# Sixteen units of a linear-attention kernel, each computed in two halves of 64 tokens instead of one of 128

## The chip, the cores and the metric

The kernel runs on one core of a Trainium2 chip. The metric is device time of one execution, in microseconds (us). The core's engines are named as the profile names them: PE (TensorE, matrix multiplication; PEld is its weight load), DVE (VectorE), ACT (ScalarE), POOL (GpSimd) and SP (SyncE, which issues most DMAs). A matmul has a stationary operand (`lhsT`, the weights loaded first) and a moving one (`rhs`); the moving operand's free size is called its columns here.

## The reference

A linear attention with a decaying state, and an ELU feed-forward layer on its output. B, H, S, D = 4, 8, 768, 48; d_model = 384, d_ff = 2048.

```python
state = np.zeros((B, H, D, D))
for t in range(S):
    kt, vt, rt = (k[:, :, t], v[:, :, t], r[:, :, t])
    cur = np.einsum('bhd,bhe->bhde', u[None] * kt, vt)
    y[:, :, t] = np.einsum('bhd,bhde->bhe', rt, state + cur)
    state = w[None, :, :, None] * state + np.einsum('bhd,bhe->bhde', kt, vt)
x = y.transpose(0, 2, 1, 3).reshape(B * S, H * D)
h = x @ w_in
g = np.where(h > 0.0, h, np.exp(np.minimum(h, 0.0)) - 1.0)
return g @ w_out
```

## The kernel before

The 768 tokens are cut into six blocks of 128 (n = 0 to 5). A block with one batch entry is a unit (n, b), so there are 24 units. The feed-forward layer takes a block of all four batch entries at once, 512 columns, in 16 steps f: `hidden` ("hid", L1031) multiplies 128 of the 2048 d_ff rows of the weights with the block's x into a PSUM tile `ps_h`, ACT and DVE make the ELU of it ("neg", "elu", "gh", "gl"), and `project` ("proj", L1075) adds its product to the output sums two steps later. Its operands are split in a high and a low part, so that a step has 9 matmuls of 512 columns for each of the two. While the steps of block n run, the units of block n + 1 are computed between them.

A unit in its closed form, for 8 heads as 4 pairs a of 2 heads i (head i of a pair lies on partitions 64i to 64i+47, `ROWS[i]`):

- scores: k times r, 128 keys by 128 queries for each head, with the decay multiplied into r (powers of w) and k (inverse powers);
- DVE copies the scores through a triangular mask (`copy_predicated`, "pa", "pb", L849) into the tile `a`, whose diagonal was laid there before by POOL ("Dp", L842) and ACT ("Eq", four instructions, L838);
- outputs y, in PSUM tiles `ps_y`: the state before the block times r, plus v times `a`; ACT and DVE split y into the high and low part of x ("xh", "xl", L949, L951);
- added state: k times v over the block's 128 tokens; DVE adds it to the decayed state ("ns", L939), which POOL had decayed ("sw", L750).

Units of blocks 2 to 5 (16 of the 24) are put on PE by `insertion` ("AY"), after "hid" and before "proj" of steps 16, 20, 23, 26, 29, 33 and so on, every fourth step to 73. Such an insertion holds the scores of one unit and the outputs and added state of the unit before; the first (step 16) holds scores alone, the last (step 77) outputs alone, and in the units of block 5 there is no added state. The strings `FIRST` and `LATER` are the order of each step; "paA+1" stands for "one step after the unit's scores", "nsY+0" for "in the step of its outputs". Every engine works off its queue in that order.

PE works with parts of its array in small matmuls: a matmul of 48 or 64 contraction rows and 32 stationary columns takes a part of 64 rows and 32 columns, and eight such parts can hold different matmuls at once. The insertion before has these groups: 32 matmuls of scores with 48 x 32 weights and 128 columns (L792); 8 of state times r, 48 x 32 and 128 columns (L807); 4 more with 128 x 32 (L812); 16 of v times `a`, 128 x 32 and 128 columns (L824); 16 of added state, 128 x 32 and 48 columns (L924). The trace has two matmul records and two weight loads for each of these fp32 matmuls, and one of each for a matmul of the feed-forward layer.

Of the kernel before, what the change touches and what calls it, by code (L numbers as in the profile page):

```python
# [8 lines left out]
F32 = mybir.dt.float32  # L9
F32R = mybir.dt.float32r  # L10
I32 = mybir.dt.int32
# [19 lines left out]
ROWS = [slice(i * DP, i * DP + D) for i in range(2)]  # L31

FILL = DP - D
Q = P // HP
W_LOW, W_HIGH = 0.8, 1.2
WARM = 7
EARLY = (0, 6)
# [29 lines left out]
class Kernel:  # L67
# [87 lines left out]
    def pair(self, a):  # L155
        return slice(a * Q, (a + 1) * Q)

# [253 lines left out]
    def stages(self, n, f):  # L411
        return [(f - t, 1, b) for b, t in enumerate(BEGIN) if n == 0 and -1 <= f - t < 4]

    def units_at(self, times, step):
        return [divmod(2 * B + j, B) for j, t in enumerate(times) if t == step]

# [11 lines left out]
    def step(self, n, f):  # L428
        nc = self.nc

        k = f + 2 if n == 0 else NF + 1
# [3 lines left out]
        last = divmod(n * NF + f - (1 if (n, f) < EARLY else 2), NF)  # L435
# [31 lines left out]
            "mr": lambda n, b: self.gather_blocks(n, b),  # L467
            "br": lambda n, b: self.decay_moved(n, b, 0),
            "bk": lambda n, b: self.decay_moved(n, b, 1),
        }  # L470
        layer = {
            "hid": lambda: self.hidden(n, f, self.rest_of(n, f)),
# [13 lines left out]
            "st": lambda: self.store(last[0]) if last[1] == NF - 1 and last[0] in self.acc else None,  # L486
            "out": lambda: self.store_next(),
            "third": lambda: self.third_slot() if (n, f) == (0, 14) else None,
            "AY": lambda: self.insertion(now),
        }  # L490
        now = n * NF + f
        for op in (LATER if n else FIRST).split():
# [3 lines left out]
            if op[-2] in "+-":  # L496
                name, times = op[:-3], {"A": SCORES, "Y": OUTPUTS, "T": TURNS}[op[-3]]
# [5 lines left out]
            name, stage = op[:-1], -1 if op[-1] == "x" else int(op[-1])  # L503
# [230 lines left out]

    def key_rest(self, n, b, eng=None):

        if n + 1 == NCH:
            return
        k = self.raw[n, b][1][:, :, 0:D]
        (eng or self.nc.gpsimd).tensor_mul(k, k, self.rev[:, :, 0:D])  # L740
        if self.general:
            self.decay_state(n, b)
# [10 lines left out]
            )  # L753

    def own_state(self, b, i):
        return self.state[b][ROWS[i], :, i * D : (i + 1) * D]

    def scores(self, n, b):
        un = self.units[n, b]
# [14 lines left out]
    def insertion(self, now):  # L774

        new, old = (self.units_at(t, now) for t in (SCORES, OUTPUTS))
        if not new:
            for at in old:
                self.outputs(*at)
            return  # L780
        nc, un = self.nc, self.units[new[0]]
        un["pa"] = [self.bank("a") for _ in range(2)]
        was = self.units[old[0]] if old else None
        if was:
            was["py"] = [
                self.ps.tile([P, T], F32, tag="h", name="ps_y", bufs=2), self.bank("y"),
            ]

        for a in range(HP):
# [6 lines left out]
        if not was:  # L796
            return
        self.by_state(*old[0])
        self.by_keys(*old[0])
        self.added_state(*old[0])  # L800
# [357 lines left out]
```

## Time and profile before

| | |
|---|---|
| time, three runs | 501.12, 502.05 and 502.75 us; median 502.05 |
| span of the profiled execution, first to last instruction | 500.2 us |
| median less that span | 1.85 us |
| PE, PEld busy | 98%, 81% of the span |
| DVE, ACT, POOL busy | 61%, 48%, 21% |
| mean granted clock of PE | 0.997 of full speed |

The profile comes from one execution, on which no other time than the span is shown; what lies around it is taken as the 1.85 us by which the median exceeds it. Busy time of PE counts the modelled length of each record, and records of matmuls overlap, so a busy PE may still be slower than it could be: start times have to be read, not only busy shares.

### The profile page before, as it was taken

To read this page: it belongs to the slowest core of one execution; us is meant where nothing else is said; L and a number is where in the kernel's file an instruction comes from. 1 tells how busy PE (TensorE), PEld (TensorE's weight loads), DVE (VectorE), ACT (ScalarE), POOL (GpSimd) and SP (SyncE) were. 2 spreads that over 40 slices of the span, in tenths; PEclk is the share of its full clock that TensorE was granted. 3 is DMA by queue.
4 is the path that set the end of the run, shared out by engine and by line. 5 is a ranking of instruction groups with operands and counts; after the bars stand their busy time and mean duration, and the time that the engine had idled before them with its cause. 6 is when DMAs were issued, how large, how long until landed. Compare 5 with 4: busy or idle time off the path is not lost.

```text
span 500.2 us, 12118 instructions
## 1 busy us (share of the span) xinstructions
PE 490.4 (98%) x5013; PEld 404.0 (81%) x5013; DVE 304.7 (61%) x533; ACT 240.9 (48%) x458; POOL 107.2 (21%) x142
## 2 busy tenths in 40 slices
PE   8999999999999999999999999999999999999995
PEld 7787778777888888888887888888878878899994
DVE  7899988875676647657556665474674343433332
ACT  3377766744445443544445435444454353444442
POOL 7623332341131331130321321301011000000000
PEclk9999999999999999999999999999999999999998
DMA  9999987483364652563523625514443000010001
GB/s 139 233 215 180 225 208 189 88 156 87 96 125 109 123 127 44 119 138 60 109 61 73 149 67 111 136 44 90 113 74 89 10 1 2 8 33 24 2 0 68
DMA packets 108453, 49.11 MB, mean 98 GB/s; under 512 B 89442, under 2 KB 104292, under 8 KB 108388
## 3 DMA queue, kind: packets, MB, share of 16 engines
q1 hardware_dynamic: 96292, 43.52, 39.6%
q10 hardware_dynamic: 12096, 4.72, 4.0%
q8 instruction: 41, 0.67, 0.6%
q14 instruction: 24, 0.20, 0.1%
HBM read 35.12 MB, written 13.11 MB: 96 GB/s over the span
## 4 chain that ended last, share of the span: by engine, by line
PE 85%; DMA 4%; DVE 4%; SPq 3%; ACT 2%; issue 1%; DVEq 0%; ACTq 0%
PE ps_acc L1075 38%; PE ps_h L1031 36%; PE ps_a L792 4%; PE ps_y L824 3%; DMA stage<-in_moe_w_out_dram 2%; PE ps_y L812 1%; SPq L212 1%; PE ps_y L924 1%; DMA stage<-in_moe_w_in_dram 1%; PE ps_y L807 1%; ACT wide L571 1%; DMA r_t<-in_r_dram 1%; SPq L169 1%; SPq L165 1%; PE ps_a L768 0%
## 5 line engine op out<-in xcount | busy, mean ns | idle before, releaser
L1031 PE MATMUL ps_h<-x,wh 128*128 128x512 f32 (+1 forms) x582 | 180.5, 391 | 1.3 <-ACT x L899 1.0
L1075 PE MATMUL ps_acc<-g,wh 128*128 128x512 f32 x480 | 165.8, 400 | 0.0
L1046 DVE SCALAR_TENSOR_TENSOR ps_h<-g,ps_h 128x512 f32<-128x512 f32 x96 | 66.8, 696 | 133.5 <-ACT g L1041 133.2
L1031 PEld LDWEIGHTS ps_h<-x,wh 128*128 128x128 f32 x582 | 108.7, 188 | 24.7 <-ACT x L899 1.3
L1040 ACT ACTIVATE g<-ps_h 128x512 f32<-128x512 f32 x96 | 57.4, 598 | 133.8 <-PE ps_h L1031 123.7
L1031 PE MATMUL ps_h<-x,wl 128*128 128x512 f32 (+1 forms) x291 | 113.9, 391 | 0.0
L1075 PEld LDWEIGHTS ps_acc<-g,wh 128*128 128x128 f32 x480 | 90.1, 188 | 21.9 <-issue 0.8
L1075 PE MATMUL ps_acc<-g,wl 128*128 128x512 f32 x240 | 93.6, 390 | 0.0
L1054 DVE SCALAR_TENSOR_TENSOR g<-ps_h,g 128x512 fp32r<-128x512 f32 x96 | 66.3, 691 | 40.2 <-ACT g L1052 35.9
L1052 ACT ACTIVATE g<-ps_h 128x512 fp32r<-128x512 f32 x96 | 57.6, 600 | 67.4 <-DVE ps_h L1046 67.2
L1031 PEld LDWEIGHTS ps_h<-x,wl 128*128 128x128 f32 x291 | 54.6, 188 | 12.7
L1041 ACT ACTIVATE g<-g 128x512 f32<-128x512 f32 x96 | 60.7, 632 | 3.0
L842 POOL TENSOR_TENSOR a<-ident,diag 128x512 f32<-128x512 f32 x20 | 20.9, 1046 | 154.2 <-PE ps_y L924 78.2
L1075 PEld LDWEIGHTS ps_acc<-g,wl 128*128 128x128 f32 x240 | 45.1, 188 | 9.0
L676 POOL TENSOR_TENSOR tb<-rk,qw 128x512 f32<-128x512 f32 x16 | 20.7, 1296 | 69.5 <-DMA rk<-blocks 53.8
L1075 PE MATMUL ps_acc<-wh,g 128*128 128x384 f32 x128 | 35.3, 339 | 0.0
L849 DVE COPY_PREDICATED a<-mask,ps_a 128x512 f32<-128x512 int32 x40 | 29.4, 734 | 0.0
L838 ACT ACTIVATE a<-ident,diag 128x128 f32<-128x128 f32 x80 | 25.4, 393 | 0.0
L1075 PEld LDWEIGHTS ps_acc<-wh,g 128*128 128x128 f32 x128 | 23.4, 187 | 1.1 <-issue 0.4
L571 ACT ACTIVATE wide<-stage 128x768 f16<-128x768 bf16 (+1 forms) x18 | 17.9, 992 | 11.2 <-DMA stage<-in_moe_w_in_dram 8.3
L949 ACT CAST x<-ps_y 128x256 fp32r<-128x256 f32 (+1 forms) x40 | 10.8, 324 | 22.8 <-DVE state L939 21.3
L1075 PE MATMUL ps_acc<-wl,g 128*128 128x384 f32 x64 | 21.6, 337 | 0.0
(114 smaller groups left out, 440.0 us busy)
## 6 DMA issues: line engine op xcount, KB each, us to landing
blocks<-tb SPq DMA_DIRECT2D x64, 128.0 KB, 2.3
rk<-blocks SPq DMA_DIRECT2D x16, 512.0 KB, 3.4
stage<-in_moe_w_out_dram SPq DMA_DIRECT2D x16, 383.8 KB, 4.1
stage<-in_moe_w_in_dram SPq DMA_DIRECT2D x64, 95.8 KB, 4.1
out_dram<-stage ACTq DMA_DIRECT2D x80, 48.0 KB, 1.7
r_t<-in_r_dram SPq DMA_DIRECT2D x17, 192.0 KB, 4.5
k_t<-in_k_dram SPq DMA_DIRECT2D x17, 192.0 KB, 5.0
v_t<-in_v_dram SPq DMA_DIRECT2D x17, 192.0 KB, 5.3
```

The source lines that it names most:

```text
L571: self.nc.scalar.activation(top.rearrange("p s (f t) -> p s f t", t=2)[..., 1], self.place(self.late, k, DEEP, i).bitcast(BF16)[..., 2], A ...
L676: (self.nc.gpsimd if i else self.nc.vector).tensor_mul(dst, src, by)
L838: self.nc.scalar.activation(un["a"][i][:, a, :], self.ident, AF.Copy, scale=diag[:, a : a + 1])
L842: self.nc.gpsimd.tensor_mul(un["a"][i], self.ident.unsqueeze(1).to_broadcast([P, HP, P]), diag.unsqueeze(2).to_broadcast([P, HP, P]),)
L849: self.nc.vector.copy_predicated(un["a"][i], self.mask.bitcast(I32).unsqueeze(1).to_broadcast([P, HP, P]), un["pa"][i].rearrange("p (a t) ...
L1031: self.nc.tensor.matmul(ph[:, part], lhsT=a[:, c * P : (c + 1) * P], rhs=x[:, c, part], start=(c == 0 and i == 0), stop=(c == NC - 1 and i ...
L1040: nc.scalar.activation(g, ph, AF.Relu, scale=-1.0)
L1041: nc.scalar.activation(g, g, AF.Exp, scale=-1.0)
L1046: self.nc.vector.scalar_tensor_tensor(ph, g, -1.0, ph, op0=ALU.add, op1=ALU.max)
L1052: nc.scalar.activation(part, g, AF.Copy, scale=W_SCALE)
L1054: nc.vector.scalar_tensor_tensor(part, g, W_SCALE, self.g[n, f][2].bitcast(F32), op0=ALU.mult, op1=ALU.subtract)
L1075: self.nc.tensor.matmul(at, lhsT=lhs, rhs=rhs, start=(f == 0 and i == 0), stop=(f == NF - 1 and i == 2),)
```

## The change

Units of blocks 2 to 5 are cut in two halves of 64 tokens. Each half has its own scores (64 keys by 64 queries) and its own state: the state before the block and, for the second half, the state after 64 tokens, without decay in between, since the decay is in r and k.

- Scores: 16 matmuls with 48 x 64 weights and 64 columns, for the 32 with 128 columns.
- Added state: one for each half, 16 matmuls with 64 x 64 weights and 48 columns, into the same PSUM banks as the scores and in the insertion of the scores, an insertion earlier than before. It is made in block 5 too.
- State times r: 32 matmuls of 48 x 32 weights and 64 columns. Half of them ("crossed") go ahead of the next unit's scores; DVE then copies one column of their result to a spare place (`self.order`), so that the other half, which adds to the same PSUM places, waits for it. The last insertion has 24 matmuls of 128 x 32 weights and 64 columns instead.
- v times `a`: 32 matmuls of 64 x 32 weights and 64 columns.
- Diagonals of both halves in one POOL instruction of 128 x 512 ("Dd"); ACT's four are gone. The masked copies take 128 x 256 each ("pd", both in the step after the scores).
- DVE makes the state after the first half ("t1", two additions of 48 x 192 elements), POOL decays it ("s2"), DVE adds the second half's ("s3"), so that two additions are new for each unit.
- POOL's product of k and the decay ("kr") moves from the step after the scores to the step before.
- Once, in step 14, `half_tables`: four PE transposes, an ACT copy of 64 x 512, four small POOL copies and two POOL memsets.

```diff
 FIRST = """
 Lq rk3 v3 Eq1 hid ns3 A1 T0 rud0 ma sum0 bkA-1 neg df0 elu sp dk0 pa1 brA-1 Y2 gh gl dr0 pb1 r4d xh2 xl2 mbT+1 mrT+1
-proj krd1 swd2 Dp0 r3 rudx rudA-2 sumA-1 wd third tT+0
+proj krd1 swd2 Dp0 r3 rudx rudA-2 sumA-1 wd third halves krA-1 tT+0
 """
 LATER = """
-hid AY tT+0 bkA-1 proj neg elu brA-1 pbA+2 gh gl st nsY+0 xhY+0 xlY+0 paA+1 EqA+1 krA+1 mbT+0 mrT+0 rudA-2
-swA+2 sumA-1 rkY+0 vY+0 DpA+0 out
+hid AY tT+0 bkA-1 proj neg elu brA-1 pdA+1 gh gl st yhY+0 ylY+0 t1A+0 s3A+2 s2A+1 krA-1 mbT+0 mrT+0 rudA-2
+sumA-1 rkY+0 vY+0 DdA+0 out
 """
...
+        for at in old:
+            self.units[at]["py"] = [
+                self.ps.tile([P, T], F32, tag="h", name="ps_y", bufs=2), self.bank("y"),
+            ]
+            if new:
+                self.by_half_states(*at, True)
+        for at in new:
+            self.scores_by_halves(*at)
+            self.added_by_halves(*at)
+        for at in old:
+            if new:
+                self.by_half_states(*at, False)
+            else:
+                self.by_whole_states(*at)
+            self.by_half_keys(*at)
...
+    def scores_by_halves(self, n, b):
+        nc, un = self.nc, self.units[n, b]
+        un["pa"] = [self.bank("a") for _ in range(2)]
         for a in range(HP):
-            for keys in (self.pair(q) for q in range(P // Q)):
+            for keys in HALVES:
                 for i, rows in enumerate(ROWS):
                     nc.tensor.matmul(
-                        un["pa"][i][keys, a * P : (a + 1) * P], lhsT=un["k"][rows, a, keys],
-                        rhs=un["r"][rows, a, :], start=True, stop=True, skip_group_check=True,
+                        un["pa"][i][keys, a * C : (a + 1) * C], lhsT=un["k"][rows, a, keys],
+                        rhs=un["r"][rows, a, keys], start=True, stop=True, skip_group_check=True,
                     )
...
+    def by_half_states(self, n, b, crossed):
+
+        un = self.units[n, b]
+        for j in range(2):
+            for a in range(HP):
+                for i, rows in enumerate(ROWS):
+                    c, g = 1 - i if crossed else i, i + j
+                    self.nc.tensor.matmul(
+                        un["py"][c][self.pair(a), g * C : (g + 1) * C],
+                        lhsT=un["S"][c][rows, a, g * Q : (g + 1) * Q],
+                        rhs=un["r"][rows, a, HALVES[c]],
+                        start=(crossed and j == 0), stop=False, skip_group_check=True,
+                    )
+        if crossed:
+            last = NC * C - 1
+            self.nc.vector.tensor_copy(self.order, un["py"][0][:, last : last + 1])
...
+    def by_half_keys(self, n, b):
+
+        un, v = self.units[n, b], self.raw[n, b][2].rearrange("p h d -> p (h d)")
+        for i, g, at, last in ((0, 0, 0, 1), (0, 1, Q, 0), (1, 1, DP - FILL, 1), (1, 2, DP + FILL, 1)):
+            for a in range(HP):
+                for c, rows in enumerate(HALVES):
+                    d = 2 * a * DP + at
+                    self.nc.tensor.matmul(
+                        un["py"][c][self.pair(a), g * C : (g + 1) * C],
+                        lhsT=v[rows, d : d + Q], rhs=un["a"][i][rows, a, :],
+                        start=False, stop=bool(last), skip_group_check=True,
+                    )
```

PE's queue from one "hid" (L1031) to the next "proj" (L1075) with an insertion of block 2 between, before; the shape is that of the output, and x32 stands for 32 matmuls in a row:

```order
L1031 MATMUL ps_h<-x,wl_139 128x512
L792 MATMUL ps_a<-stage,tb 32x128 x32
L807 MATMUL ps_y<-stage,state_60 32x128 x8
L812 MATMUL ps_y<-stage,state_60 32x128 x4
L824 MATMUL ps_y<-a,stage 32x128 x16
L924 MATMUL ps_y<-stage 32x48 x16
L1075 MATMUL ps_acc_1707<-g_1923,wh_136 128x512
```

The same place after the change (lines have new numbers: hid L1183, proj L1227, scores L891, added state L903, state times r L919, v times `a` L948); the two left-out pieces are 14 more matmuls each of L919, which alternate between the two states:

```order
L1183 MATMUL ps_h<-x,wl_139 128x512
L919 MATMUL ps_y<-stage,state_59 32x64
L919 MATMUL ps_y<-stage,state_60 32x64
...
L891 MATMUL ps_a<-stage,tb 64x64 x16
L903 MATMUL ps_a<-v_t_73,k_t_72 64x48 x16
L919 MATMUL ps_y<-stage,state_60 32x64
L919 MATMUL ps_y<-stage,state_59 32x64
...
L948 MATMUL ps_y<-a,stage 32x64 x32
L1227 MATMUL ps_acc_1723<-g_1961,wh_136 128x512
```

An insertion of 76 matmuls has become one of 96, of which no matmul has more than 64 columns; the scores now stand behind half of the previous unit's state products, and the added state is that of the new unit.

DVE's queue around an insertion, before, from "gl" of the step ahead (L1054) over the unit's diagonal sum (L733) and the block transposes of the next unit's r and k (L640) to the first masked copy of the scores (L849):

```order
L1054 SCALAR_TENSOR_TENSOR g_1966<-ps_h,g_1964 128x512
L733 TENSOR_REDUCE diag<-ru 128x8
L640 STREAM_TRANSPOSE tb<-r_t_68 128x4x4x32
L640 STREAM_TRANSPOSE tb<-k_t_69 128x4x4x32
L1046 SCALAR_TENSOR_TENSOR ps_h<-g,ps_h 128x512
L1054 SCALAR_TENSOR_TENSOR g_2083<-ps_h,g_2081 128x512
L939 TENSOR_TENSOR state_60<-sw,ps_y 48x4x48 x2
L951 TENSOR_TENSOR x<-ps_y,x 128x2x128
L951 TENSOR_TENSOR x<-ps_y,x 128x128
L1046 SCALAR_TENSOR_TENSOR ps_h<-g,ps_h 128x512
L1054 SCALAR_TENSOR_TENSOR g_2130<-ps_h,g_2128 128x512
L849 COPY_PREDICATED a<-mask,ps_a 128x512
```

And after the change (gl is L1206, the sum L762, the copy to `order` L927, the transposes L669, elu L1198, the low part of x L845, the half state L795, the masked copies L831):

```order
L762 TENSOR_REDUCE diag<-ru 128x8
L927 COPY stage<-ps_y 128x1
L669 STREAM_TRANSPOSE tb<-r_t_68 128x4x4x32
L669 STREAM_TRANSPOSE tb<-k_t_69 128x4x4x32
L1198 SCALAR_TENSOR_TENSOR ps_h<-g,ps_h 128x512
L1206 SCALAR_TENSOR_TENSOR g_2138<-ps_h,g_2136 128x512
L845 TENSOR_TENSOR x<-ps_y,x 128x3x64 x2
L795 TENSOR_TENSOR state_60<-state_61,ps_a 48x4x48 x2
L1198 SCALAR_TENSOR_TENSOR ps_h<-g,ps_h 128x512
L831 COPY_PREDICATED a<-stage,ps_a 128x256 x2
```

The copy to `order`, which waits for PE's crossed matmuls, stands ahead of the transposes and the step's elu; the two additions of the state now follow the split of y, and both masked copies come one step after the scores.

## Rows read from the trace of the kernel before

**Rows 1.** The page's first part: busy time of each engine, share of the span, instructions.

```profile
PE 490.4 (98%) x5013; PEld 404.0 (81%) x5013; DVE 304.7 (61%) x533; ACT 240.9 (48%) x458; POOL 107.2 (21%) x142
```

**Rows 2.** The page's chain that ended last, shares of the span by engine.

```profile
PE 85%; DMA 4%; DVE 4%; SPq 3%; ACT 2%; issue 1%; DVEq 0%; ACTq 0%
```

**Rows 3.** Timeline of one insertion: start us, length, engine, line, operation, records.

```profile
272.39 0.69 DVE L1054 SCALAR_TENSOR_TENSOR g<-ps_h,g 128x512 fp32r<-128x512 f32 x1
273.00 0.54 DVE L733 TENSOR_REDUCE diag<-ru 128x8 f32<-128x384 f32 x1
...
273.45 1.30 DVE L640 STREAM_TRANSPOSE tb<-stage 128x512 f32<-128x512 f32 x2
273.77 1.16 PE L792 MATMUL ps_a<-stage,tb 48*32 48x128 f32 x61
...
274.67 0.28 PE L807 MATMUL ps_y<-stage,state 48*32 48x128 f32 x3
...
275.16 0.42 PE L812 MATMUL ps_y<-stage,state 128*32 128x128 f32 x8
275.17 0.70 DVE L1046 SCALAR_TENSOR_TENSOR ps_h<-g,ps_h 128x512 f32<-128x512 f32 x1 [0.41 <-ACT g L1041]
275.40 1.06 PE L824 MATMUL ps_y<-a,v_t 128*32 128x128 f32 x32
...
276.27 0.52 PE L924 MATMUL ps_y<-v_t,k_t 128*32 128x48 f32 x32
276.53 0.69 DVE L1054 SCALAR_TENSOR_TENSOR g<-ps_h,g 128x512 fp32r<-128x512 f32 x1 [0.66 <-ACT g L1052]
...
276.73 0.50 PE L1075 MATMUL ps_acc<-g,wh 128*128 128x512 f32 x1
...
278.91 0.63 PE L1031 MATMUL ps_h<-x,wh 128*128 128x512 f32 x2
```

**Rows 4.** Windows, PE alone: sum over the 12 insertions with both units and added state.

```profile
128.37:131.54 3.17, 3.17 (x153) 1.00 0.28 66
...
sum 35.26, PE 35.26; mean PE 2.94
```

**Rows 5.** Windows, PE alone: sum over the three insertions without added state.

```profile
sum 7.72, PE 7.72; mean PE 2.57
```

**Rows 6.** Timeline of PE: the first insertion (scores alone) and what follows.

```profile
110.20 1.21 PE L792 MATMUL ps_a<-stage,tb 48*32 48x128 f32 x64
111.33 0.51 PE L1075 MATMUL ps_acc<-g,wh 128*128 128x512 f32 x1
```

**Rows 7.** Timeline of PE: the last insertion (outputs alone) and what follows.

```profile
410.75 0.45 PE L807 MATMUL ps_y<-stage,state 48*32 48x128 f32 x16
411.13 0.43 PE L812 MATMUL ps_y<-stage,state 128*32 128x128 f32 x8
...
412.36 0.51 PE L1075 MATMUL ps_acc<-g,wh 128*128 128x512 f32 x1
```

**Rows 8.** Timeline of PE: added states of three early units in a row, 48 columns.

```profile
30.00 0.55 PE L924 MATMUL ps_st<-v_t,k_t 128*32 128x48 f32 x32
30.37 0.89 PE L924 MATMUL ps_st<-raw 128*32 128x48 f32 x64
31.19 0.50 PE L1075 MATMUL ps_acc<-g,wh 128*128 128x512 f32 x1
```

**Rows 9.** Records of one line: count, shortest, median, longest ns, starts, forms.

```profile
L792 PE MATMUL ps_a<-stage,tb x1024: 269/269/295, 110.2 to 392.3; 48*32 48x128 f32 x171
```

**Rows 10.** The same for the added state.

```profile
L924 PE MATMUL ps_y<-v_t,k_t x384: 203/206/230, 47.5 to 335.7; 128*32 128x48 f32 x192
```

**Rows 11.** Timeline of PE: eight transposes like those of `half_tables`, and what follows.

```profile
52.15 0.60 PE L628 MATMUL ps_rT<-ident,r_t 128*128 128x128 f32 x4
...
52.94 0.48 PE L1075 MATMUL ps_acc<-g,wh 128*128 128x512 f32 x1
```

**Rows 12.** Groups by line: count, busy us, mean ns of one, idle before.

```profile
L849 DVE COPY_PREDICATED a<-mask,ps_a 128x512 f32<-128x512 int32 x40 | 29.4, 734 | 0.0
L838 ACT ACTIVATE a<-ident,diag 128x128 f32<-128x128 f32 x80 | 25.4, 393 | 0.0
L939 DVE TENSOR_TENSOR state<-sw,ps_y 48x192 f32<-48x192 f32 x32 | 11.0, 345 | 0.4
```

**Rows 13.** Timeline of DVE at the start of the insertion at 128.37 us.

```profile
128.20 0.54 DVE L733 TENSOR_REDUCE diag<-ru 128x8 f32<-128x384 f32 x1
```

More of the change, by code (lines that the diff above doesn't have):

```diff
@@ L34 @@
 Q = P // HP
+C = P // 2
+HALVES = [slice(c * C, (c + 1) * C) for c in range(2)]
 W_LOW, W_HIGH = 0.8, 1.2
@@ L412, in stages, with half_tables @@
         return [(f - t, 1, b) for b, t in enumerate(BEGIN) if n == 0 and -1 <= f - t < 4]
+    def half_tables(self):
+        nc = self.nc
+        ps = self.bank("pt")
+        for a in range(HP):
+            nc.tensor.transpose(ps[:, a * P : (a + 1) * P], self.qw[:, a, :], self.ident)
+        nc.scalar.copy(self.rev[0:C].rearrange("p h d -> p (h d)"), ps[0:C])
+        at = 3 * 2 * DM + HP * P
+        t = self.late.bitcast(F32).rearrange("p s d w -> p (s d w)")[:, at : at + P + 1]
+        self.ident_c, self.mask_c, self.order = t[:, 0:C], t[:, C:P], t[:, P : P + 1]
+        for rows in HALVES:
+            nc.gpsimd.tensor_copy(self.ident_c[rows], self.ident[rows, rows])
+            nc.gpsimd.tensor_copy(self.mask_c[rows], self.mask[rows, rows])
+        self.spares = [
+            self.wk.tile([P, HP, 2 * D], F32, tag="vd", name="state", bufs=2) for _ in range(2)
+        ]
+        for t in self.spares:
+            nc.gpsimd.memset(t, 0.0)
     def units_at(self, times, step):
@@ new lines, in decay_half_state, with next_state @@
+    def decay_half_state(self, n, b):
+        if n + 1 == NCH:
+            return
+        un = self.units[n, b]
+        un["sw"] = self.wk.tile([P, HP, D], F32, tag="sw", name="sw", bufs=1)
+        for i, rows in enumerate(ROWS):
+            self.nc.gpsimd.tensor_mul(
+                un["sw"][rows], self.own(un["S"][1], i),
+                self.pw[rows, :, P : P + 1].to_broadcast([D, HP, D]),
+            )
+    def next_state(self, n, b):
+        if n + 1 == NCH:
+            return
+        un = self.units[n, b]
+        self.state[b] = self.spares.pop(0)
+        for i, rows in enumerate(ROWS):
+            self.nc.vector.tensor_add(self.own(self.state[b], i), un["sw"][rows], un["ps"][1][rows])
@@ new lines, in diag_by_halves, with take_by_halves @@
+    def diag_by_halves(self, n, b):
+        un = self.units[n, b]
+        a = self.wk.tile([P, 2, HP, C], F32, tag="a", name="a", bufs=1)
+        un["a"] = [a[:, i] for i in range(2)]
+        self.nc.gpsimd.tensor_mul(
+            a.rearrange("p i a t -> p a i t"),
+            self.ident_c.unsqueeze(1).unsqueeze(1).to_broadcast([P, HP, 2, C]),
+            un["diag"].rearrange("p (a i) -> p a i", i=2).unsqueeze(3).to_broadcast([P, HP, 2, C]),
+        )
+    def take_by_halves(self, n, b):
+        un = self.units[n, b]
+        for i in range(2):
+            self.nc.vector.copy_predicated(
+                un["a"][i], self.mask_c.bitcast(I32).unsqueeze(1).to_broadcast([P, HP, C]),
+                un["pa"][i][:, 0 : HP * C].rearrange("p (a t) -> p a t", a=HP),
+            )
@@ L758, in scores, with split_halves @@
+    def split_halves(self, n, b, i):
+        nc, un = self.nc, self.units[n, b]
+        for c, py in enumerate(un["py"]):
+            at = b * P + c * C
+            x = self.x_of(n)[:, :, :, at : at + C]
+            y = py[:, 0 : NC * C].rearrange("p (g t) -> p g t", t=C)
+            if i == 0:
+                nc.scalar.copy(x[:, 0], y)
+            else:
+                nc.vector.tensor_sub(x[:, 1], y, x[:, 0].bitcast(F32))
     def scores(self, n, b):
@@ L776, in insertion @@
         new, old = (self.units_at(t, now) for t in (SCORES, OUTPUTS))
[L777 to L785, printed above, removed]
+        old = [at for at in old if at[0] > 1]
+        for at in old:
+            self.units[at]["py"] = [
                 self.ps.tile([P, T], F32, tag="h", name="ps_y", bufs=2), self.bank("y"),
@@ L799, in insertion, with added_by_halves @@
-        self.by_keys(*old[0])
-        self.added_state(*old[0])
+                        un["pa"][i][keys, a * C : (a + 1) * C], lhsT=un["k"][rows, a, keys],
+                        rhs=un["r"][rows, a, keys], start=True, stop=True, skip_group_check=True,
+                    )
+    def added_by_halves(self, n, b):
+        nc, un = self.nc, self.units[n, b]
+        kr, v_t = self.raw[n, b][1], self.v_of(n, b)
+        at = HP * C
+        for a in range(HP):
+            for i in range(2):
+                for c, rows in enumerate(HALVES):
+                    nc.tensor.matmul(
+                        un["pa"][c][HALVES[i], at + a * D : at + (a + 1) * D],
+                        lhsT=kr[rows, 2 * a + i, :], rhs=v_t[rows, 2 * a + i, :],
+                        start=True, stop=True, skip_group_check=True,
+                    )
+        un["ps"] = [
+            pa[:, at : at + HP * D].rearrange("p (a c) -> p a c", a=HP) for pa in un["pa"]
+        ]
@@ new lines, in by_whole_states @@
+    def by_whole_states(self, n, b):
+        un = self.units[n, b]
+        for c in range(2):
+            for g in range(NC):
+                for a in range(HP):
+                    self.nc.tensor.matmul(
+                        un["py"][c][self.pair(a), g * C : (g + 1) * C],
+                        lhsT=un["S"][c][:, a, g * Q : (g + 1) * Q],
+                        rhs=un["r"][:, a, HALVES[c]],
+                        start=(g == 0), stop=False, skip_group_check=True,
+                    )
```

34 lines of the change are left out of this document (29 added, 5 removed).

## The prediction

> **What bounds the kernel now.** I read the busy shares first: PE is busy for 490.4 of 500.2 us, no other engine for more than 61% [rows 1]. The chain that ended last says the same from the other side: 85% of it is PE [rows 2]. So time is PE's time, and other engines matter only where they make PE wait. The change touches no matmul of the feed-forward layer, only the insertions between "hid" and "proj". How long those are I read from start to start, first matmul of an insertion to the next one of "proj", since lengths of records overlap: 12 insertions with both units and added state take 35.26 us, 2.94 each [rows 4]; three without added state 7.72 us, 2.57 each [rows 5]; the first 111.33 - 110.20 = 1.13 [rows 6]; the last 412.36 - 410.75 = 1.61 [rows 7]. Together 45.7 us, 9% of the span, and that is all that the change can act on.
>
> **What a small matmul costs.** Within one insertion the starts are 273.77 (scores), 274.67, 275.16, 275.40, 276.27 and 276.73 [rows 3]. v times `a` is 16 matmuls, 32 records, in four strips of 32 stationary columns: eight rounds of four in 0.87 us, so 0.109 us for a round of 128 columns. The added states at 30.00 are 96 records, 24 rounds of 48 columns, in 1.19 us [rows 8]. The last insertion shows what a change of the array's division costs: 16 records in eight parts are two rounds, 0.22, but the matmuls with 128 rows start 0.38 after them [rows 7]; the change is 0.16. Taking 0.16 from the 1.19 leaves 0.043 for a round of 48 columns, and between the two a round of 64 columns is 0.056.
>
> Adding up the insertion of before in this way tests the method: scores 8 x 0.109, state in eight parts 2 x 0.109, change 0.16, state in four strips 2 x 0.109, v times `a` 8 x 0.109, added state 8 x 0.043, change 0.16: 2.84. Measured are 2.94. The missing 0.10 is in the matmuls with eight parts: scores and state to 275.16 take 1.39 [rows 3], where rounds and the change give 1.25. So matmuls in eight parts run late by more than their columns say. The 32 of the scores take 0.90 us, 0.028 each.
>
> That lateness is the open price, since the change puts 64 of 96 matmuls in eight parts with half the columns. Two ends. By columns alone nothing is late: eight matmuls are two rounds, 0.111, or 0.014 each. By count alone each matmul costs the 0.028 that it costs now, whatever its columns. I take a value between: if a later matmul cannot be taken in before an old one has ended, the cost goes with how long a matmul stays. Its two records stay a round and one record: 0.109 + 0.269 = 0.378 us at 128 columns [rows 9]; at 64 columns 0.056 + 0.219 = 0.275, the 0.219 being interpolated between 0.206 at 48 [rows 10] and 0.269. 0.028 x 0.275 / 0.378 = 0.0204 us.
>
> A rule of the Trainium skill speaks against the whole change, and the rows against the rule. The page TensorE: Matmul & The Clock Gate, section "Wait — 56ns, not 53.3ns?", says that starts of matmuls are never less than about 25 ns apart, however few columns they have. By it (an estimate) 192 records would take 4.8 us for an insertion. But it would also give 3.8 for the 152 records of before, which take 2.94; in parts of the array the rule does not hold here.
>
> **The change part by part, on PE.** One insertion now: crossed state products 16 x 0.0204 = 0.33; change of division 0.16; scores in four parts, 16 matmuls, eight rounds of 0.056 = 0.45; added state in the same parts, eight rounds of 0.043 = 0.34; change 0.16; the other state products 0.33; v times `a` 32 x 0.0204 = 0.65; change to "proj" 0.16. Sum 2.58.
>
> - 12 insertions: 2.58 - 2.94 = -0.36 each, -4.3 us.
> - Three with units of block 5: 2.58 - 2.57, nothing; there the added state is new work.
> - The first: 0.45 + 0.34 + 0.16 = 0.95 for 1.13, -0.2.
> - The last: 24 matmuls in four strips, 12 rounds of 0.056 = 0.67, change 0.16, v times `a` 0.65, change 0.16, 1.64 for 1.61: +0.03.
> - `half_tables`: four transposes on PE; eight take 52.94 - 52.15 = 0.79 [rows 11], so +0.4.
>
> Sum -4.0 us. The profiled execution's span of 500.2 becomes 496.2; with the 1.85 us that lie around it, which is how far the median of the runs is above it, 498.0.
>
> **The other engines**, costed at nothing, with their cover:
>
> - DVE: two masked copies of 0.734 [rows 12] shrink to between half and all of that; two additions of 0.345 are new. Between nothing and +0.7 us for a unit, which has four steps of PE time, 15 us or so; DVE is busy for 61%.
> - ACT loses 4 x 0.393 for a unit. POOL's work stays but for "kr", one step earlier and also in block 5; it is 21% busy.
> - The copy to `order` is the one new wait of PE. It stands behind DVE's sum, which in the closest case ends at 128.74, 0.37 after the insertion's start [rows 13, 4]. The crossed products are done at 0.33 + 0.22 = 0.55. The copy itself lies between nothing and the 0.345 of a whole addition, so the wait is over by 0.9. PE asks for it after crossed, scores, added state and two changes, at 1.44. Cover 0.5 us.
> - Behind that copy on DVE stand the two transposes (1.30 us) and the step's "elu". It starts 275.17 - 273.77 = 1.40 after the insertion today, then 0.9 + 1.3 = 2.2 [rows 3]. "gl" would end 0.8 later than now (276.53 + 0.69, 3.45 after the start), at 4.25. It frees the `ps_h` that the next "hid" needs; that starts at 278.91 now, 5.14 after, and would at 4.78. Cover 0.5 again. If the insertion were 0.4 shorter still, the cover would be 0.1.
>
> **The rivals.**
>
> 1. *Columns alone.* Nothing is late: 0.22 + 0.16 + 0.45 + 0.34 + 0.16 + 0.22 + 0.45 + 0.16 = 2.16. Then 12 x -0.78, 3 x -0.41, -0.18, -0.17 (the last: 0.67 + 0.16 + 0.45 + 0.16 = 1.44) and +0.4: -10.5 us, 491.5. For it: the added states in four strips run at their columns for 96 records. Against it: eight parts don't, even with 128 columns.
> 2. *Count of matmuls (slower).* Each matmul keeps its 0.028, so that 96 of them and three changes are 3.17: 12 x 0.23 + 3 x 0.60 - 0.07 + 0.28 + 0.4 = +5.2 us, 507.2. It decides from a cost of 0.0245 for a matmul in eight parts on (2.84 for an insertion: 12 x -0.10 + 3 x 0.27 + 0.4 is nothing). For it: 0.028 is the only price in eight parts that the trace has. Against it: 48 columns in four strips cost 0.021 a matmul. The Trainium skill has this as a rule, in TensorEngine Tiling (Array Packing), "Instruction Overhead": about 60 cycles for every matmul, so one should not take a tiling factor from a dimension that is already small.
> 3. *The new wait binds.* The copy to `order` comes more than 0.5 us late, because DVE is still with the step before. Each further 0.3 us costs 15 x 0.3 = 4.5, and the time is about 502.5. Against it: the closest case above.
> 4. *No change.* A price near 0.0245: 502.
>
> **How the numbers follow.** The forecast, 495 to 500.4, has 0.56; columns alone 0.17; count 0.12; the wait 0.05; no change 0.10. The likeliest time is 498.0. From 492 to 504 leaves out about 2 in 10: the far side of columns alone and of count. A difference of 0.3% (1.5 us) is about what a measurement of this kernel can tell from none. Faster by more takes nearly all of the forecast and all of columns alone, 0.71; within it no change, half the wait and the edge of the forecast, 0.15; slower the rest, 0.14.
>
> **What would show it.** Insertions with both units near 2.58 from start to start, of which crossed and uncrossed products take 0.3 each and v times `a` 0.65; near 2.16 or 3.17 the rivals. Scores plus added state of 0.8. No idle PE before the uncrossed products or before "hid" after an insertion; such a wait, named DVE, is rival 3. I would be wrong altogether if a change of division between parts of 64 x 32 and 64 x 64, which no row of before has, cost more than 0.16, or nothing (2 x 0.16 x 15, 4.8 us).

## The result, and the profile after

The changed kernel takes 506.25 us (median of 5 runs, 505.44 to 508.79), the kernel before 502.73 beside it (5 runs, 501.12 to 503.94): 1.0086 times as long, 95% interval 1.0059 to 1.0113. It is slower, where 498.0 was forecast and 492 to 504 given as the range. The profiled execution has a span of 504.2 us, 4.0 more than before, at a mean clock of 0.997 as before.

The page after: busy times (to be held against [rows 1]), the DMA queue that carries instructions, and the chain (against [rows 2]).

```profile
PE 489.0 (97%) x5769; PEld 402.7 (80%) x5769; DVE 308.0 (61%) x580; ACT 222.1 (44%) x395; POOL 118.5 (24%) x152
...
q8 instruction: 47, 0.77, 0.6%
...
PE 89%; DVE 3%; SPq 2%; DMA 2%; issue 2%; ACT 1%; ACTq 0%; DVEq 0%
```

PE's busy time fell by 1.4 us while the span grew by 4.0, so PE stands idle more. The view of PE's waits says where (columns: PE, tile, line, what it waited for: us in total, times, longest). L948 is v times `a`, L1227 "proj", L919 the products with the states. Lines of the changed kernel are not those of before.

```profile
PE ps_y L948 <- issue: 4.6, 4, 1.6
...
PE ps_y L919 <- DVE g L1206: 0.5, 1, 0.5
PE ps_acc L1227 <- issue: 0.4, 1, 0.4
```

"Issue" means that nothing in the profile was waited for. Four such waits, 0.8 to 1.6 us of idle PE each, lie inside v times `a`, and one of 0.4 in "proj"; PE's waits of before have none of this kind. The windows of the insertions, from start to start as in [rows 4 to 7], PE alone (columns: length, busy time and records, granted clock, DMA share, GB/s):

```profile
110.32:111.40 1.08, 1.08 (x65) 1.00 0.08 15
128.45:131.93 3.48, 2.93 (x193) 1.00 0.14 33
144.59:147.32 2.73, 2.73 (x194) 1.00 0.03 8
159.98:163.62 3.64, 2.83 (x194) 1.00 0.15 37
176.27:180.71 4.44, 2.86 (x193) 1.00 0.31 80
197.51:201.26 3.75, 2.92 (x194) 1.00 0.17 41
...
276.38:278.97 2.59, 2.59 (x193) 1.00 0.03 6
295.78:298.50 2.72, 2.72 (x193) 1.00 0.02 6
...
393.64:397.98 4.34, 2.98 (x194) 1.00 0.02 6
414.78:416.46 1.68, 1.68 (x114) 1.00 0.03 10
sum 48.96, PE 43.83; mean PE 2.58
```

Ten of the 15 long insertions take 2.59 to 2.73 us, together 26.55. Five take 3.48 to 4.44, of which PE is busy for 2.83 to 2.98. The sum is 48.96, for 45.7 before and 41.3 in the forecast.

An insertion without a stop, PE's timeline (start, length, line, operation, records):

```profile
276.38 0.46 PE L919 MATMUL ps_y<-stage,state 48*32 48x64 f32 x32
276.77 0.69 PE L891 MATMUL ps_a<-stage,tb 48*64 48x64 f32 x32
277.28 0.63 PE L903 MATMUL ps_a<-v_t,k_t 64*64 64x48 f32 x32
277.85 0.45 PE L919 MATMUL ps_y<-stage,state 48*32 48x64 f32 x32
278.11 0.93 PE L948 MATMUL ps_y<-a,v_t 64*32 64x64 f32 x64
278.97 0.51 PE L1227 MATMUL ps_acc<-g,wh 128*128 128x512 f32 x1
```

From start to start: crossed products 0.39, scores 0.51, added state 0.57, uncrossed 0.26, v times `a` 0.86; 2.59. And one with a stop, with DVE's copy to `order` (L927):

```profile
176.85 0.16 DVE L927 COPY stage<-ps_y 128x1 f32<-128x1 f32 x1
...
177.73 0.45 PE L919 MATMUL ps_y<-stage,state 48*32 48x64 f32 x32
...
178.00 0.57 PE L948 MATMUL ps_y<-a,v_t 64*32 64x64 f32 x26
...
180.15 0.63 PE L948 MATMUL ps_y<-a,v_t 64*32 64x64 f32 x38 [1.58 <-issue]
180.15 0.47 PEld L948 LDWEIGHTS ps_y<-a,v_t 64*32 64x32 f32 x37 [1.75 <-issue]
...
180.71 0.50 PE L1227 MATMUL ps_acc<-g,wh 128*128 128x512 f32 x1
```

The weight loads stop too, in the middle of a run of equal instructions whose first 26 needed nothing new. The copy is done at 177.01, 0.72 before the products that wait for it. What does lie there is a transfer of the instruction queue (DMA view of the stretch 177.7 to 178.9; columns: packets, MB, share):

```profile
q8 instruction: 1, 0.02, 4.8%
```

Counting PE's records from the program's start gives the pattern. All are counted, weight loads, matmuls and the waits of its sequencer (55 of the first 4033). The stops of the trace after, all of them that are "issue", with their length from the start of the last matmul ahead to the start of the next; the idle time in it is 0.2 to 0.4 us less:

| stop, us | length | PE records before it | transfer starts, lands | PE goes on after landing | after its start |
|---|---|---|---|---|---|
| 161.95 | 1.03 | 4033 = 15 x 256 + 193 | 160.65, 161.60 | 1.37 | 2.32 |
| 178.35 | 1.80 | 4545 = 17 x 256 + 193 | 177.82, 178.75 | 1.40 | 2.33 |
| 199.55 | 1.04 | 5057 = 19 x 256 + 193 | 197.82, 199.14 | 1.45 | 2.77 |
| 377.02 | 0.75 | 9921 = 38 x 256 + 193 | 375.35, 376.23 | 1.54 | 2.42 |
| 396.17 | 1.57 | 10433 = 40 x 256 + 193 | 395.36, 396.40 | 1.34 | 2.38 |

Every one stands at the same place of a block of 256 records, and the queue makes one transfer of 16 KB for every 256. While each of the five transfers ran, the DMA views show no other packet, so none was held up by other traffic. The trace before has 41 transfers and one stop at such a place, 0.19 us, in its longest insertion, 128.37 ([rows 4], 3.17). Hence theory 1: **PE runs out of instructions.** A fp32 matmul is four of them, so an insertion is now 384 in 2.6 us where it was 304 in 2.94; 256 last about 1.75 us instead of 2.5, while a block can be used only 2.3 to 2.8 us after its transfer starts. Theory 2: the data of v times `a` (`a` itself, or a PSUM place) come late, and the profile fails to name the releaser.

The same count shows which insertions are hit. In the five, PE had entered the block within a microsecond of the insertion's start (160.09, 176.45, 197.63, 374.51, 394.43), the transfer of the next block started 0.2 to 1.4 us after that, and PE had begun its 256 within 1.7 to 2.5 us. Three other blocks were used up as fast, in 1.72 to 1.82 us (entered at 144.63, 218.10 and 237.47), and PE did not stop behind them: there the next transfer had started 2.5 to 3.9 us before PE entered the block, while the step ahead still ran.

### The profile page after: what moved, and what is told of

It reads as the page before. It is cut to its first block, busy times and chain, and to the rows that moved or that the text cites. A ratio compares the mean times of both kernels' runs of the same rounds, so it can differ in the third digit from the quotient of the medians.

```text
span 504.2 us, 13606 instructions
## 1 busy us (share of the span) xinstructions
PE 489.0 (97%) x5769; PEld 402.7 (80%) x5769; DVE 308.0 (61%) x580; ACT 222.1 (44%) x395; POOL 118.5 (24%) x152
## 4 chain that ended last, share of the span: by engine, by line
PE 89%; DVE 3%; SPq 2%; DMA 2%; issue 2%; ACT 1%; ACTq 0%; DVEq 0%
PE ps_acc L1227 39%; PE ps_h L1183 38%; PE ps_y L948 3%; PE ps_y L919 2%; PE ps_a L891 2%; PE ps_a L903 1%; DMA stage<-in_moe_w_out_dram 1%; SPq L214 1%; PE ps_a L857 1%; DMA r_t<-in_r_dram 1%; SPq L171 1%; SPq L167 1%; PE ps_y L976 1%; DVE g L1206 0%; DMA w_col<-in_w_dram 0%
## 5 line engine op out<-in xcount | busy, mean ns | idle before, releaser
L1183 PE MATMUL ps_h<-x,wh 128*128 128x512 f32 (+1 forms) x582 | 180.6, 391 | 1.2 <-ACT x L1051 0.9
L1227 PE MATMUL ps_acc<-g,wh 128*128 128x512 f32 x480 | 165.8, 400 | 0.0
L1198 DVE SCALAR_TENSOR_TENSOR ps_h<-g,ps_h 128x512 f32<-128x512 f32 x96 | 66.4, 692 | 128.9 <-ACT g L1193 128.6
L1192 ACT ACTIVATE g<-ps_h 128x512 f32<-128x512 f32 x96 | 57.5, 599 | 165.3 <-PE ps_h L1183 149.6
L1183 PEld LDWEIGHTS ps_h<-x,wh 128*128 128x128 f32 x582 | 108.6, 188 | 24.5 <-ACT x L1051 1.2
L1183 PE MATMUL ps_h<-x,wl 128*128 128x512 f32 (+1 forms) x291 | 113.9, 391 | 0.0
L1227 PEld LDWEIGHTS ps_acc<-g,wh 128*128 128x128 f32 x480 | 90.1, 188 | 21.6 <-issue 0.4
L1227 PE MATMUL ps_acc<-g,wl 128*128 128x512 f32 x240 | 93.7, 390 | 0.4 <-issue 0.4
L1206 DVE SCALAR_TENSOR_TENSOR g<-ps_h,g 128x512 fp32r<-128x512 f32 x96 | 66.2, 690 | 37.7 <-ACT g L1204 36.6
L1183 PEld LDWEIGHTS ps_h<-x,wl 128*128 128x128 f32 x291 | 54.6, 188 | 12.8
L1227 PEld LDWEIGHTS ps_acc<-g,wl 128*128 128x128 f32 x240 | 45.1, 188 | 9.8 <-issue 0.8
L822 POOL TENSOR_TENSOR a<-stage,diag 128x512 f32<-128x512 f32 x16 | 16.7, 1046 | 82.5 <-PE ps_y L948 59.4
L1227 PE MATMUL ps_acc<-wh,g 128*128 128x384 f32 x128 | 35.3, 339 | 0.0
L1227 PEld LDWEIGHTS ps_acc<-wh,g 128*128 128x128 f32 x128 | 23.4, 187 | 1.2 <-issue 0.4
L769 POOL TENSOR_TENSOR k_t<-k_t,rev 128x384 f32<-128x384 f32 x11 | 14.6, 1328 | 36.2 <-DVE ru L753 36.2
L1227 PE MATMUL ps_acc<-wl,g 128*128 128x384 f32 x64 | 21.6, 337 | 0.0
L620 POOL CAST wh<-stage 128x384 fp32r<-128x384 f32 x16 | 8.6, 538 | 54.2 <-DVE stage L609 54.2
L609 DVE SCALAR_TENSOR_TENSOR stage<-stage,wide 128x768 int32<-128x768 int32 (+1 forms) x18 | 16.2, 901 | 0.2
```

The lines of the kernel that those rows point to most:

```text
L609: self.nc.vector.scalar_tensor_tensor(low, low, 13, self.place(self.wide, k, WIDE, i), op0=ALU.logical_shift_right, op1=ALU.bitwise_or,)
L822: self.nc.gpsimd.tensor_mul(a.rearrange("p i a t -> p a i t"), self.ident_c.unsqueeze(1).unsqueeze(1).to_broadcast([P, HP, 2, C]), un["dia ...
L1183: self.nc.tensor.matmul(ph[:, part], lhsT=a[:, c * P : (c + 1) * P], rhs=x[:, c, part], start=(c == 0 and i == 0), stop=(c == NC - 1 and i ...
L1192: nc.scalar.activation(g, ph, AF.Relu, scale=-1.0)
L1198: self.nc.vector.scalar_tensor_tensor(ph, g, -1.0, ph, op0=ALU.add, op1=ALU.max)
L1206: nc.vector.scalar_tensor_tensor(part, g, W_SCALE, self.g[n, f][2].bitcast(F32), op0=ALU.mult, op1=ALU.subtract)
```

## The experiments

**Shift the boundaries: `e1_shift`.** In `half_tables`, ahead of the copy on ACT:

```diff
+        for _ in range(44):
+            nc.tensor.matmul(
+                ps[C : C + Q, 0:4], lhsT=self.ident[:, 0:Q], rhs=self.ident[:, 0:4],
+                start=True, stop=True, skip_group_check=True,
+            )
```

> The changed kernel with 44 small extra matmuls (176 PE instructions; 128 x 32 weights, 4 columns, results unused) in half_tables, so that every later PE instruction stands 176 places further on. Theory 1 (instruction supply): in the changed kernel PE stops inside v times a near 162, 178, 200 and 396 us, each time where 256 more of its records have run, and a 16 KB instruction transfer landed 1.4 us before it goes on; shifted by 176, the stops move to other insertions: none near 396, and about 1 us each in some 6 to 10 of the insertions between 128 and 275 us; the time is 1 to 5 us above the changed kernel's. Theory 2 (data: the masked copies, v or a PSUM bank come late in those units): the same four insertions, at the same units, take 3.6 to 4.4 us from start to start, whatever stands before them, and the time is that of the changed kernel plus the extra matmuls, 1 to 3 us.

Measured: 520.12 us (516.68 to 521.22), before 501.85 (500.86 to 504.19) beside it, 1.0345 (1.0315 to 1.0375). Its waits, where L953 is v times `a` and L1232 "proj":

```profile
PE ps_y L953 <- issue: 11.2, 9, 1.6
...
PE ps_acc L1232 <- issue: 0.8, 1, 0.8
```

The stops moved: ten of 0.9 to 1.8 us, the first at 137.55 (record 3265 = 12 x 256 + 193), the last at 314.33 (7873 = 30 x 256 + 193), in ten insertions in a row, and none where they were at 377 and 396. Data are where they were, so theory 2 falls. (A further one, 0.3 us of idle PE at 23, lies at record 705 = 2 x 256 + 193, ahead of the added matmuls.) The time is far over what was expected. By the starts of the steps, the profiled execution's span of 519.3 us is 15.1 over that of the changed kernel: 4.6 us are the added matmuls and a slower clock behind them, some 9 the ten stops, less the five of the changed kernel, with another stretch of slow clock, and 1.4 waits of this execution in its first 60 us. The clock (windows, columns as above; 1.00 is 2.4 GHz, 0.50 is 1.2):

```profile
108.40:112.40 4.00, 4.00 (x13) 0.57 0.77 139
171.20:173.60 2.40, 0.78 (x33) 1.00 0.62 162
173.70:177.00 3.30, 3.30 (x9) 0.50 0.35 96
```

It fell after the tiny matmuls, and again after a stop of 1.84 us; after the stop of 1.80 in the changed kernel it stayed at 1.00 (180.2 to 184), as it did after one of 1.80 here, at 210.35. Why one and not the others is open.

**The supply by itself: `e3_burst`.** The kernel before, with 256 small matmuls (1024 instructions) that wait for nothing, behind "third" of step 14:

```diff
+    def burst(self):
+        ps = [self.bank("pt") for _ in range(2)]
+        for j in range(256):
+            i, a = j % 2, j // 2 % HP
+            self.nc.tensor.matmul(
+                ps[i][self.pair(a), 0 : P // 2], lhsT=self.ident[ROWS[i], 0:Q],
+                rhs=self.mask[ROWS[i], 0 : P // 2], start=True, stop=True, skip_group_check=True,
+            )
```

> The kernel before with 256 extra matmuls (1,024 PE instructions) in a row in step 14, 48 x 32 weights, 64 columns, eight parts of the array, operands that never change, no wait between them; results unused. Theory 1: PE stops at every 256th record, and a block of 256 takes 2.3 to 3 us, so that the burst takes 9 to 12 us. If small matmuls only cost their issue and columns (0.0139 to 0.0204 us each), the burst takes 3.6 to 5.2 us without a stop. The price of the prediction for matmuls in eight parts with 64 columns, 0.0204, is read from its pieces between the stops.

Measured, one execution: 516.37 us. The burst in PE's timeline (L1041 is "hid" behind it), and below it the burst's window (columns as above):

```profile
103.25 1.96 PE L418 MATMUL ps_pt<-mask,ident 48*32 48x64 f32 x169
108.04 1.67 PE L418 MATMUL ps_pt<-mask,ident 48*32 48x64 f32 x128 [2.83 <-issue]
111.77 2.08 PE L418 MATMUL ps_pt<-mask,ident 48*32 48x64 f32 x128 [2.06 <-issue]
115.22 1.56 PE L418 MATMUL ps_pt<-mask,ident 48*32 48x64 f32 x87 [1.38 <-issue]
116.71 1.22 PE L1041 MATMUL ps_h<-x,wh 128*128 128x512 f32 x2
...
103.25:116.70 13.45, 7.19 (x513) 0.73 0.55 85
```

Between stops stand exactly 128 matmul records, so 256 instructions. PE uses them up in 1.7 to 2.1 us, and the next come 3.73 and 3.45 us after the last (108.04, 111.77, 115.22). The burst takes 13.46 us, where its matmuls need 5.3 at the price of its first piece (some 84 matmuls in 1.75 us, 0.0207 each, against the prediction's 0.0204). Supply alone makes the stops, in a kernel without the change. The burst was longer than expected for two reasons. A block comes 2.3 to 2.9 us after its transfer starts, about as beside the insertions, but that transfer starts only 1.1 to 1.4 us after PE has entered the block ahead (at 105.11 for 103.70, 109.36 for 108.04, 112.90 for 111.77). And the granted clock was 0.50 from 109.51 on, until 119.75, so that the last pieces ran slower.

**Give the supply time: `e2_split_all` and `e4_split_some`.** The uncrossed products and v times `a` move behind "proj", as an operation of their own, "AZ"; in all 15 insertions (the condition is then `bool(new)`), or only in steps 26, 29, 33, 69 and 73, those with a stop in the trace after, as shown:

```diff
-hid AY tT+0 bkA-1 proj neg elu brA-1 pdA+1 gh gl st yhY+0 ylY+0 t1A+0 s3A+2 s2A+1 krA-1 mbT+0 mrT+0 rudA-2
+hid AY tT+0 bkA-1 proj AZ neg elu brA-1 pdA+1 gh gl st yhY+0 ylY+0 t1A+0 s3A+2 s2A+1 krA-1 mbT+0 mrT+0 rudA-2
...
+        self.insertion_rest(now, False)
+
+    def insertion_rest(self, now, late):
+
+        new, old = (self.units_at(t, now) for t in (SCORES, OUTPUTS))
+        old = [at for at in old if at[0] > 1]
+        if late != (now in (26, 29, 33, 69, 73)):
+            return
```

> The changed kernel with each insertion in two: crossed state products, scores and added state before proj as now, the other state products and v times a behind proj. No burst of small matmuls is longer than 192 PE instructions. Theory 1 (instruction supply): no stop over 0.3 us in any insertion; one more change of division each, about 0.25 us x 15 = +3.8, against some 6 us of stops that go: 503 to 505 us, 2 to 3 under the changed kernel. Theory 2 (data that come late in four units): those waits shrink too, since v times a comes 2 us later, so the time alone does not tell; a wait left over would be named by DVE or DMA.

Measured: 503.84 us (502.50 to 506.39), 1.0055 (1.0037 to 1.0073).

> The changed kernel with only five insertions in two (steps 26, 29, 33, 69 and 73: the four that stop, and the one after which proj stops). Theory 1: these lose their stops, about 6.2 us in all, for five more changes of division, 1.3 us; if the few semaphore instructions that the split adds do not shift the others into a stop: 500.5 to 502.5 us, 4 to 5 under the changed kernel and about that of the kernel before. Theory 2: the same or less, as in the run with all of them split.

Measured: 500.69 us (499.13 to 501.44), 0.9977 (0.9967 to 0.9986); both ratios are against the 501.85 above. Neither trace has an "issue" stop of PE from the first insertion on. PE's timeline of the split insertion that lay at 176.27, from `e2_split_all` (L928 states, L900 scores, L912 added state, L1236 "proj", L957 v times `a`, L1192 "hid"):

```profile
175.65 0.45 PE L928 MATMUL ps_y<-stage,state 48*32 48x64 f32 x32
...
176.59 0.66 PE L912 MATMUL ps_a<-stage 64*64 64x48 f32 x31
177.19 0.50 PE L1236 MATMUL ps_acc<-g,wh 128*128 128x512 f32 x1
...
179.46 0.45 PE L928 MATMUL ps_y<-stage,state 48*32 48x64 f32 x32
179.73 0.93 PE L957 MATMUL ps_y<-a,v_t 64*32 64x64 f32 x64
180.59 0.73 PE L1192 MATMUL ps_h<-x,wh 128*128 128x512 f32 x2
```

All the same instructions, no stop. A split costs about 0.23 us, put down to one more change of the array's division (the ten that `e2_split_all` has more cost 2.26 from the fourth "hid" to the last); five cost less than the stops that they remove.

**Is it pace or place? `e6_before_shift` and `e7_shift_split`.** The 44 matmuls of `e1_shift`, once in the kernel before, behind "third" of step 14, and once in the changed kernel with all insertions split:

```diff
-proj krd1 swd2 Dp0 r3 rudx rudA-2 sumA-1 wd third tT+0
+proj krd1 swd2 Dp0 r3 rudx rudA-2 sumA-1 wd third shift tT+0
```

> Kernel: the one before the change, with 44 matmuls of four columns (176 TensorE instructions, results unused) ahead of step 15, which moves every later boundary of 256 instructions by 176 places. Theory of supply: an insertion of before has 304 instructions in 2.94 us, 256 of them in about 2.5 us, close to the 2.3 to 2.8 us that one block takes to arrive; so the moved boundaries give stops of at most .2 to .5 us in some insertions, and the kernel is slower by what the added matmuls take themselves (1 to 3 us by the same addition to the changed kernel, where it took 2.9) and at most 2 us more: 502.5 to 507. If the stops belong to any insertion whose boundary falls early, whatever its pace: ten stops of 1 to 1.8 us, as in the changed kernel with the same addition, and 515 to 520.

Measured: 506.65 us (505.05 to 507.23), before 501.53 beside it, 1.0091 (1.0074 to 1.0109). Two stops lie at the boundary, 0.51 us at 241.40 (record 5825 = 22 x 256 + 193) and 0.79 at 320.05 (7617 = 29 x 256 + 193); the second in PE's timeline, where L933 is the added state:

```profile
319.74 0.52 PE L933 MATMUL ps_y<-stage 128*32 128x48 f32 x30
320.84 0.24 PE L933 MATMUL ps_y<-stage 128*32 128x48 f32 x2 [0.58 <-issue]
```

Steps 13 and 14, with the addition and its slow clock, are 4.7 us longer than before, and all steps behind them together 1.1, the two stops. The second is longer than the 0.5 us expected at most. So the insertion of before is close to the edge and barely over it: the same shift gave the changed kernel ten stops, this one two.

> Kernel: the changed one with both the 44 added matmuls (results unused) and all 15 insertions split behind the projection. Theory of supply: the split spreads the instructions so that no block of 256 is used up before the next has come, wherever the boundaries lie; no stop over .3 us in an insertion, and of the 18.3 us that the addition cost the changed kernel only its own 2.9 us and the slower clock right behind it stay: 503.8 + 3 to 5, so 506.5 to 509. If the addition costs by something else than the stops (the clock, the place of later work), the time stays at 515 to 520.

Measured: 507.52 us (507.01 to 508.50), 1.0122 (1.0107 to 1.0137): 3.7 over `e2_split_all`, the price of the addition, with no stop. So a long stop needs both: the pace of the insertion, and a place of the boundaries by which a block begins near the insertion's start. Splitting takes away the pace, and the stops went with the boundaries in either place.

**The small wait: `e5_later_state` and `e8_early_state`.** The insertion at 128.45 waits for something else, gl (L1206) of the step before, since one of the two banks of `ps_y` is the `ps_h` that gl reads. Both kernels have the split of `e4_split_some`. One puts the additions that make the next state ("s3") to the end of the step, the other, shown here, between elu and gl:

```diff
-hid AY tT+0 bkA-1 proj AZ neg elu brA-1 pdA+1 gh gl st yhY+0 ylY+0 t1A+0 s3A+2 s2A+1 krA-1 mbT+0 mrT+0 rudA-2
+hid AY tT+0 bkA-1 proj AZ neg elu brA-1 s3A+2 pdA+1 gh gl st yhY+0 ylY+0 t1A+0 s2A+1 krA-1 mbT+0 mrT+0 rudA-2
```

> Kernel: the one with five insertions split, and in blocks 2 to 5 the two vector additions that make the next state (L816, .72 us) stand at the end of the step's vector work instead of ahead of the sum of the decays and of elu. Theory of supply of instructions: nothing changes in it, since TensorE's order is that of the split kernel; no stop over .3 us behind an instruction transfer. Theory of the small wait: the .75 us that the insertion at 128.8 waits for gl of the step before comes from those additions standing ahead of elu; without them there the wait shrinks below .2 us and the kernel takes .4 to .8 us less than the split kernel's 500.7, so 499.9 to 500.3. Rival to the small wait's cause: gl is late because of ScalarE or of the hidden layer's products alone; then the wait stays at .6 to .8 us and the time stays at 500.5 to 500.9.

Measured: 501.02 us (500.39 to 502.94), before 501.53, 0.9992 (0.9982 to 1.0001). A miss: the wait, from start to start of the matmuls around it, went from 0.75 to 0.64. DVE in `e4_split_some` ahead of that insertion shows why:

```profile
124.92 0.69 DVE L1215 SCALAR_TENSOR_TENSOR g<-ps_h,g 128x512 fp32r<-128x512 f32 x1 [0.66 <-ACT g L1213]
125.52 0.73 DVE L817 TENSOR_TENSOR state<-sw,ps_a 48x192 f32<-48x192 f32 x2
126.28 0.56 DVE L754 TENSOR_TENSOR ru<-stage 128x384 f32<-128x384 f32 x1
126.87 0.56 DVE L758 TENSOR_TENSOR ru<-ru,u_b 128x384 f32<-128x384 f32 x1
127.47 0.69 DVE L1207 SCALAR_TENSOR_TENSOR ps_h<-g,ps_h 128x512 f32<-128x512 f32 x1
...
128.83 0.69 DVE L1215 SCALAR_TENSOR_TENSOR g<-ps_h,g 128x512 fp32r<-128x512 f32 x1
```

The additions (L817), put behind the two others, still stand ahead of elu (L1207), on which gl (L1215) hangs. The order of the three hardly matters, their sum does.

> Kernel: the one with five insertions split, with the two vector additions of the next state (L817, .73 us) between elu and gl of the same step, where VectorE stands idle for .66 us while ScalarE works, instead of behind gl. Theory of the small wait: at the second insertion gl is late because three operations, those additions (.73) and two of .56, stand between one gl and the next elu, .95 us more than ScalarE's work takes; putting the additions behind those two moved nothing, since they still stood ahead of the next elu. Ahead of gl they fill idle time, so gl comes .7 us earlier, the wait of .75 us at the insertion near 128.8 goes, and the kernel takes .5 to .8 us less than the 500.7 of the split kernel, in profile steps 2 to 94 as well. Rival: GpSimd's decayed state (sw) isn't there so early, VectorE waits for it ahead of gl and the insertion waits as long as before or longer; then 500.5 to 502. Supply of instructions: TensorE's order is unchanged, so no stop over .3 us behind an instruction transfer.

Measured: 500.47 us (499.76 to 501.81), before 501.57 beside it, 0.9975 (0.9960 to 0.9990). DVE now:

```profile
125.87 0.73 DVE L817 TENSOR_TENSOR state<-sw,ps_a 48x192 f32<-48x192 f32 x2
126.63 0.69 DVE L1215 SCALAR_TENSOR_TENSOR g<-ps_h,g 128x512 fp32r<-128x512 f32 x1
...
128.30 0.69 DVE L1207 SCALAR_TENSOR_TENSOR ps_h<-g,ps_h 128x512 f32<-128x512 f32 x1
```

The additions lie ahead of gl, where DVE waited 0.66 us for ACT, and the next elu starts 1.67 us after gl instead of 2.55. The wait is gone, and the step with that insertion takes 7.03 us instead of 7.83 (hid to hid). In the time this can't be seen against `e4_split_some`: 500.47 lies between the range of the theory and that of its rival. The profiled execution is 2.0 us late by its fourth "hid" already, ahead of all this, 1.4 of it in a step in which its granted clock was 0.50 (26.97 to 30.39; `e4_split_some` has 1.00 there), and such differences are larger than the gain. From the fourth "hid" to the last the spans are 441.9 before, 446.2 after, 441.1 with five splits and 440.1 with this. Both of the last two beat both kernels, by about a quarter of a per cent the kernel before.

## Why the prediction was wrong

The step that failed is the first one, "So time is PE's time, and other engines matter only where they make PE wait", and with it the sum "Sum 2.58" for one insertion: it priced the array's work, and had no term, and no rival, for the supply of instructions. In its place the runs showed five stops of 0.75 to 1.80 us, each where the next block of 256 instructions had not come. The counts were there to ask about it, 304 instructions in [rows 4]'s 2.94 us, and a change that makes them 384 in 2.58; the time that a block takes was not among the rows, though the trace of before has it (a transfer started at 128.54, its block was begun 2.62 us later).

- *Matmul in eight parts, 0.0204 us, and the insertion of 2.58.* Right in the price and the sum. Undisturbed insertions take 2.59 to 2.73, mean 2.655; the burst gives 0.0207. Part by part the sum is less good: scores and added state came out 0.06 and 0.07 higher than 0.45 and 0.50 with the change, v times `a` 0.05 higher than 0.81, crossed and uncrossed products 0.10 and 0.07 lower than 0.49 and 0.33. That these cancel is luck. "Columns alone" (2.16) and "count" (3.17) are both refuted. That the time ended near the latter's 507.2 is chance. Four of the ten undisturbed insertions take about 0.13 us more than the rest, all of it in v times `a`; the cause is open.
- *The 25 ns between starts* of the Trainium skill's page TensorE: Matmul & The Clock Gate, "Wait — 56ns, not 53.3ns?", stays contradicted for parts of the array: 192 records in 2.59 us are 13.5 ns each.
- *First, last and `half_tables`.* 1.08 for 0.95, 1.68 for 1.64, and four transposes with 0.36 in their own step for 0.4. Right but for +0.13.
- *"The other engines, costed at nothing."* True of the copy to `order`, the wait that was feared: it is over 0.7 us early. Not true once of DVE: the "two additions of 0.345" made gl late for the insertion at 128.45, 0.76 us, shown by `e8_early_state`. They were put against four steps of PE time; in the early units there are three, and two other operations stand beside them.
- *The missing term.* Five stops. Account of the span: forecast -4.0; the five disturbed insertions take 19.65 us instead of 5 x 2.655, +6.4 with the small wait in it; the stop in "proj" of step 69, +0.6; the 15 insertions at 2.655 instead of 2.58, +1.1; first and last, +0.2. That gives +4.3, and measured is +4.0.

Not all of the 4 us was to be had without the stops. The splits cost 5 x 0.23, the tables 0.4, and the plain insertions give 15 x 2.655 for 42.98, -3.2: with the small wait left in, about 0.8 us better than before by the steps, as `e4_split_some` has it.

## What to carry to other kernels

Where a change cuts work into more, smaller matmuls, count PE's instructions in each burst as well as their time: here 256 in 2.5 us passed with a stop of at most 0.8, and 256 in 1.7 to 1.9 us stopped PE for up to 1.8 where the block had been entered inside the burst, although the page's busy share of the instruction queue is 0.6%. A wait "issue" in the middle of equal instructions, at multiples of 256 records, with a 16 KB transfer of the instruction queue just ahead, was that here and no late operand. The remedy is long instructions in between, put only where a boundary falls badly, since a switch of the array's division costs too; and every edit that adds instructions anywhere ahead moves all the boundaries.

## What the runs showed of the hardware

- PE's instructions come in blocks of 256, one transfer of 16 KB each. PE goes on 1.3 to 1.5 us after a late one has landed and 2.3 to 2.8 us after it started in the changed kernel (1.2 to 1.5 and 2.2 to 2.7 in the ten stops of `e1_shift`), and in the burst every 3.5 to 3.7 us. In the five stops the transfer for the next block started when 91 to 229 records of the present one were left (at 177.82, 4454 had begun, and the block ended with the 4545th). In these traces the crossing of a boundary is hidden for the feed-forward matmuls and, but for 0.2 us, for the insertion before. For 256 instructions in 1.7 to 1.9 us it is hidden where the next transfer started 2.5 us or more before the block was entered, and not where it started after. The Trainium skill, Runtime: NRT & Kernel Launch, section "Instruction fetch mechanics", has the blocks of 16 KiB and 256 instructions and says that crossing a boundary is mostly hidden; the traces agree on the blocks, and on the second but for these stops.
- The granted clock fell from 1.00 to 0.50 (2.4 to 1.2 GHz) after the 44 tiny matmuls in all three kernels that have them (in `e1_shift` from 108.83 to 112.25, where the added matmuls and the slow clock together cost 4.6 us); after one stop of 1.84 us (173.69 to 177.10); and in the burst of `e3_burst`, behind a stop of 3.04 us from start to start (109.51 to 119.75).
